# Two forms of the first weights instead of three, and gaps between the operands of the first layer

## The chip, the cores and the metric

The kernel runs on one core of one Trainium2 chip. The metric is the device time of one execution in microseconds (us). An execution under the hardware profiler also gives a span, the time from its first to its last recorded instruction, and the start and the duration of every instruction.

## The reference

A causal convolution over the sequence, with one softmax-normalised kernel of 7 taps for each of 8 heads, and behind it a layer of two matrix products with a hardswish between them. Everything is float32.

```python
# x (8, 4096, 192), weight (8, 7), w_in (192, 2048), w_out (2048, 192)
w = softmax(weight, axis=-1)
y = causal_conv(x, w).reshape(32768, 192)     # 7 taps, one w row per head
h = y @ w_in                                  # 32768 x 2048
g = h * clip(h + 3, 0, 6) / 6
out = g @ w_out                               # 32768 x 192
```

## The kernel before

The 32768 tokens are worked through in 32 blocks of 1024. A block has a convolution (VectorE, ScalarE and a DMA that adds), a **first layer** (`y @ w_in` and the gate) and a **second layer** (`g @ w_out`, done with sums and products of half matrices in place of some of the plain products). In the steady state TensorE does the first layer of a block, then its second layer, then the next block's first layer; the convolution and the splitting of the next block go on beside it.

**The first layer's products.** A tile `y` has 64 channels in its lower 64 partitions for one half of the tokens and the same 64 channels in its upper 64 partitions for the other half, three such thirds `s` side by side, 512 tokens each. So one step of the contraction is a *pair* of matmuls, `k = 0, 1`, one on rows 0 to 63 and one on rows 64 to 127 of TensorE's array, each with its own weights load (64 rows by 128 columns) and 512 columns of `y`. `products` (L437) issues them.

The matmuls run in float32r, a float32 form that goes once over the columns. To keep float32's accuracy both operands are split: `high_of` (L424) writes `y * CUT` in float32r, `low_of` (L427) the rest of it; for the weights, `Rounding.part` (L226) writes `high` (ScalarE, `sig * CUT`), `full` (GpSimd, a cast of `sig`) and `low` (GpSimd, `sig - high`). Three passes then make one product: weights HIGH with columns HIGH, LOW with HIGH, and FULL with LOW (`PASSES`, L28). A *unit* (L465) is one tile of 128 hidden channels for 1024 tokens: 3 passes by 3 thirds by 2 = 18 matmuls, then `relu` on ScalarE (L316) and `gate` on VectorE (L320). A block has 16 units, so 288 matmuls or 144 pairs. Units 0 to 7 take their columns from `y_own`, units 8 to 15 from `y_other`, a copy of `y_own` with the two halves of the partitions exchanged, which four DMAs of SyncE's queue make (`swap`, L303).

**The tiles.** `w_in_parts` (L122) are three tiles of 8 x 3 x 128 floats to a partition (12,288 bytes each). `y_own` are two tiles, HIGH and LOW, of 3 x 512 floats (6,144 bytes each), and `y_other` is one tile with the same two inside it. In the program's allocation they begin at 82,080, 94,368 and 106,656 (weights), 159,648 and 165,792 (`y_own`) and 171,936 (`y_other`) bytes into the partition: each of them is 160 modulo 256, and so is each step by `c`, `s` or part inside them, since 512, 2,048 and 6,144 are multiples of 256. The tag `other` serves `z_other`, three sums of the second layer (L656), in turn with `y_other`. The last tile ends 64 bytes short of the end of the partition.

**Where the weights are made.** At the start, 16 `Rounding` units turn the float64 bits of `w_in` and `w_out` into float32. Eight of them, the ones for `w_in`, end in `part`. This runs beside the first layer of block 0, up to about 62 us.

**The second layer** (`second_layer`, L559) issues float32 matmuls of 256 or 512 columns on the four column groups of the array, each with a weights load of 32 columns (`matmul`, L582).

Of the kernel before, what the change touches and what calls it, by code (L numbers as in the profile page):

```python
# [11 lines left out]
F32 = mybir.dt.float32  # L12
# [5 lines left out]


CUT = 1.0 - 2.0**-13  # L20
HIGH, LOW, FULL = range(3)

PASSES = (HIGH, HIGH), (LOW, HIGH), (FULL, LOW)  # L28


@with_exitstack
def kernel(
# [8 lines left out]
    nc = tc.nc  # L41
    P = nc.NUM_PARTITIONS
# [6 lines left out]
    N = 512  # L49
# [3 lines left out]
    K3 = D // D2  # L53
# [7 lines left out]
    NP = NC // 2  # L61
# [5 lines left out]
    cst = ctx.enter_context(tc.tile_pool(name="cst", bufs=1))  # L67
    xs = ctx.enter_context(tc.tile_pool(name="xs", bufs=1))
    ys = ctx.enter_context(tc.tile_pool(name="ys", bufs=1))
    yo = ctx.enter_context(tc.tile_pool(name="yo", bufs=1))  # L70
# [23 lines left out]
    for base, dma in ((0, nc.scalar), (D2, nc.sync)):  # L94
        dma.dma_start(
            out=w_sb[base : base + D2],
            in_=weight.unsqueeze(1).to_broadcast([H, GJ, KC]),
# [21 lines left out]
    nc.vector.memset(zeros, 0.0)  # L119


    w_in_parts = [cst.tile([P, NP, K3, P], F32, name=f"w_in{n}") for n in range(3)]  # L122
    def own_tiles(name):
        return [yo.tile([P, K3, N], F32, name=f"{name}{n}", tag=f"y{n}") for n in range(2)]

    sm = yo.tile([P, 1], F32, name="sm")
    y_own, z_early = own_tiles("y"), []

    def other_tile():
        return yo.tile([P, 2, K3, N], F32, name="y_other", tag="other")  # L130

    y_other = [other_tile()]
    w_out = cst.tile([P, NP, 7, DH], F32, name="w_out")
    B11, B12, B21, B22, T1, T2, T4 = range(7)
# [38 lines left out]
    class Rounding:  # L173
# [51 lines left out]

        def part(self):  # L226
            if len(self.dst) > 1:
                high, low, full = self.dst
                nc.scalar.mul(r32(high), self.sig[:], CUT)
                nc.gpsimd.tensor_copy(out=r32(full), in_=self.sig[:])  # L230
                nc.gpsimd.tensor_tensor(  # L231
                    out=r32(low), in0=self.sig[:], in1=high, op=ALU.subtract
                )

    def r32(ap):
        return ap.bitcast(F32R)
# [21 lines left out]
    for n in range(5):  # L258
# [7 lines left out]
        out=e_sb[:], in0=w_sb[:], in1=mx[:].to_broadcast([P, KC]), op=ALU.subtract  # L266
# [9 lines left out]
    y = ys.tile([P, K3, N], F32, name="y")  # L276
    OWN, OTHER = range(2)

    def conv_units(i, parts, cuts=1):


        x = x_tiles.pop(i)
        W = N // cuts

        def tap(part, k, t):
            c = c_sb[:, k : k + 1]
            to = y[:, part, t : t + W]
            if k == 0:
                nc.vector.tensor_scalar(
                    out=to, in0=x[:, part, t : t + W], scalar1=c, scalar2=None, op0=ALU.mult  # L290
                )
            else:
                nc.vector.scalar_tensor_tensor(
                    out=to, in0=x[:, part, k + t : k + t + W], scalar=c, in1=to,
                    op0=ALU.mult, op1=ALU.add,
                )

        return [
            lambda part=part, k=k, t=t: tap(part, k, t)
            for part in parts for k in range(KC) for t in range(0, N, W)  # L300
        ]

    def swap(to, part):  # L303
        nc.sync.dma_start(out=to[D2:P], in_=part[0:D2])
        nc.sync.dma_start(out=to[0:D2], in_=part[D2:P])
# [118 lines left out]
    def high_of(out, x):  # L424
        nc.scalar.mul(r32(out), x, CUT)

    def low_of(out, x, high, engine):  # L427
        engine.tensor_tensor(out=r32(out), in0=x, in1=high, op=ALU.subtract)
# [3 lines left out]
    def swap_parts(thirds=slice(0, K3)):  # L432
        y_other[0] = other_tile()
        for n in range(2):
            swap(y_other[0][:, n, thirds], y_own[n][:, thirds])

    def products(n, slot, s, steps=range(3), begin=False, end=False):  # L437
        group, c = divmod(n, NP)
        for m_ in steps:
            wn, yn = PASSES[m_]  # L440
            for k in range(2):
                r = slice(k * D2, (k + 1) * D2)
                nc.tensor.matmul(  # L443
                    out=psum[:, 2 * slot + k], lhsT=r32(w_in_parts[wn][r, c, s]),
                    rhs=r32(y_other[0][r, yn, s] if group else y_own[yn][r, s]),
                    start=begin and m_ == 0, stop=end and m_ == 2, skip_group_check=True,
                )

# [14 lines left out]
    def first_layer(i, jobs):  # L463

        def unit(n):  # L465
            slot = free_slots.pop(0)
            for m_ in range(3):
                for s in range(K3):
                    products(n, slot, s, (m_,), s == 0, s == K3 - 1)
            to, both = places(n, slot)  # L470
            relu(to, both)
            gate(to, both)
            free_slots.append(slot)
# [50 lines left out]
    TH = N // 2  # L524
# [34 lines left out]
    def second_layer(i, between):  # L559
        last = i + 1 == NB  # L560
        ours = [free_slots.pop(0) for _ in range(3)]
        d, e, b, c, a, x_ = (psum[:, 2 * n + k] for n in ours for k in range(2))
# [87 lines left out]
        f, h = ends  # L650
# [2 lines left out]
        A2, B2, C2 = a[second, lo], a[third, lo], a[first, lo]  # L653
        T_2, T_4 = x_[second], e[first]
        A, B, V = f[fourth], h[fourth], b[fourth]
        z_other = yo.tile([P, 3, NP // 2, TH], F32, name="z_other", tag="other")  # L656
        sums_a12 = z_other[:, 0], z_other[:, 1], z_other[:, 2], z[:, :, 1]

        def sum_a12(n):
# [44 lines left out]
        t = clock[2]  # L704
# [204 lines left out]
    with tc.manual_schedule():  # L909
# [4 lines left out]
            out=c_sb[:], in0=e_sb[:], in1=sm[:].to_broadcast([P, KC]), op=ALU.mult  # L914
# [3 lines left out]
        thirds = [slice(s, s + 1) for s in range(K3)]  # L918
# [10 lines left out]
        b, b1 = (2 * free_slots[-1] + k for k in range(2))  # L929
        for _ in range(3):  # L930

            nc.tensor.matmul(  # L932
                out=psum[:, b], lhsT=zeros[:, 0:P], rhs=zeros, start=True, stop=True
# [10 lines left out]
        def thirds_of(n, *which, end=False):  # L944
            if n not in early:
                early[n] = free_slots.pop(0)
            for s in which:
                products(n, early[n], s, begin=s == pe_third, end=end)

        def high_y(s, of):  # L950
            high_of(y_own[HIGH][:, thirds[s]], of)
            swap(y_other[0][:, HIGH, thirds[s]], y_own[HIGH][:, thirds[s]])

        def low_y(s, of):
            low_of(y_own[LOW][:, thirds[s]], of, y_own[HIGH][:, thirds[s]], nc.vector)
            swap(y_other[0][:, LOW, thirds[s]], y_own[LOW][:, thirds[s]])

        def all_of(s):
            return y[:, thirds[s]]
# [7 lines left out]
        for u in conv0[5 : per - 3]:  # L967
            u()
        join(0)
        high_y(pe_third, psum[:, b : b + 1])  # L970
        part(0)
        for u in conv0[per - 3 : per]:
            u()
        low_y(pe_third, psum[:, b : b + 1])
        high_y(0, all_of(0))
        low_y(0, all_of(0))
        thirds_of(0, pe_third, 0)
        thirds_of(NP, pe_third)
        split(1)
        clamp(1)  # L980
        for u in conv0[per + 2 : per + 2 * pe_taps]:
            u()
        add(y[:, 1], psum[:, b1], y[:, 1])
        high_y(1, all_of(1))
        join(1)
        part(1)
        low_y(1, all_of(1))
        for n in (5, 6, 7, 8):
            load(n)
# [36 lines left out]
        for r in range(2 * NP):  # L1026
            k = order[r]
            if k in early:
                slot = early[k]
                if k == NP:  # L1030
                    thirds_of(k, 1, end=True)
            else:
                slot = free_slots.pop(0)
                for m_ in range(3):
                    for s in range(K3):
                        products(k, slot, s, (m_,), s == 0, s == K3 - 1)
            to, both = places(k, slot)
            relu(to, both)
            n = joins.get(r)
# [62 lines left out]
        begin_block_two()  # L1102
        direct_out(0, *third)
        swap_parts()
        w_sums(((T3, B22, B12),))
        last = ctx.enter_context(tc.tile_pool(name="last", bufs=1, reuse_waits="tile"))
# [6 lines left out]
        for i in range(1, NB):  # L1113
            jobs = dict(zip((3, 6, 9, 12), ([job] for job in conv[3:7])))
            jobs[-1] = left
            if i > 1 and conv:

                jobs[-1] = left[:2] + conv[1:2] + left[2:]
                jobs[1] = conv[2:3]
            first_layer(i, jobs)  # L1120
            for job in conv[7:]:
                job()
            conv = []

            def begin_conv():
                x_tiles[i + 2] = load_x(i + 2)
                conv.extend(conv_jobs(i + 2, True))

            between = []
            if i + 1 < NB:  # L1130
                between = [(52.4, split_high), (63, split_rest), (64.2, swap_parts)]
            if i + 2 < NB:
                between += [(40, begin_conv), (65, lambda: conv[0]())]
            left = second_layer(i, between)
# [33 lines left out]
```

## Time and profile before

| | us |
|---|---|
| time, median of 3 runs | 2195.64 |
| lowest and highest of the 3 | 2195.4, 2195.95 |
| time of the profiled execution | 2195.4 |
| its span | 2193.6 |
| TensorE busy | 2185.0 (100%) |
| TensorE's weight loads busy | 1564.3 (71%) |
| VectorE busy | 1979.9 (90%) |
| ScalarE busy | 1271.8 (58%) |
| GpSimd busy | 1018.1 (46%) |

Line numbers (L443) are those of the kernel before. `PE` is TensorE's matmuls, `PEld` its weight loads, `DVE` VectorE, `ACT` ScalarE, `POOL` GpSimd, `SP` SyncE. In a line of groups, the last figures are the busy time, the mean duration of one in ns, and the idle time of the engine just before, with what ended it. A matmul's duration includes its way through the array, so durations of neighbours overlap; how fast the matmuls go is read from the distance between their starts.

### The profile page before, as it was taken

Reading aid. Unit: us, or ns where it says so; the run is one execution under the profiler, and the core shown is the slowest. Engines: PE = TensorE matmul, PEld = TensorE weight load, DVE = VectorE, ACT = ScalarE, POOL = GpSimd, SP = SyncE. Lnnn points to the kernel's source line nnn. Section 1 sums busy time; section 2 is a strip of 40 time slices with the busy share of each in tenths; the row PEclk is TensorE's granted clock in tenths of the full one; section 3 lists DMA queues with packets and bytes.
Section 4 is the critical chain, followed back from the end, with each engine's and each line's share of the span. In section 5 each row is a group of like instructions: output and inputs, shape, how many; then the busy total and the mean of one; then the engine's idle time right before and its main releaser. Section 6 shows DMA issues by size and latency. Waiting matters only on the chain.

```text
span 2193.6 us, 53710 instructions
## 1 busy us (share of the span) xinstructions
PE 2185.0 (100%) x23086; PEld 1564.3 (71%) x23086; DVE 1979.9 (90%) x1871; ACT 1271.8 (58%) x1761; POOL 1018.1 (46%) x867
## 2 busy tenths in 40 slices
PE   9999999999999999999999999999999999999998
PEld 5577777777777777777777777777777777777776
DVE  8889899889899898998989988999999999898987
ACT  7456565565655665555656556565566555565644
POOL 4545543355433555334554335553355543455433
PEclk9999999999999999999999999999999999999999
DMA  7366556756567665666655675656666566765564
GB/s 166 66 120 98 97 99 111 128 90 107 97 111 121 103 109 91 110 112 120 98 97 100 112 127 90 107 98 112 121 106 106 91 110 112 122 97 97 99 105 64
DMA packets 329821, 231.80 MB, mean 106 GB/s; under 512 B 208816, under 2 KB 293296, under 8 KB 329584
## 3 DMA queue, kind: packets, MB, share of 16 engines
q0 software_dynamic: 98752, 122.35, 36.6%
q1 hardware_dynamic: 229320, 105.73, 23.8%
q8 instruction: 181, 2.97, 0.6%
q10 hardware_dynamic: 1512, 0.30, 0.1%
q14 instruction: 56, 0.46, 0.1%
HBM read 31.72 MB, written 25.17 MB: 26 GB/s over the span
## 4 chain that ended last, share of the span: by engine, by line
PE 98%; ACT 1%; DVE 0%; POOL 0%; DMA 0%; issue 0%; POOLq 0%; DVEq 0%
PE psum L583 49%; PE psum L443 47%; PE psum L331 2%; PE psum L924 0%; PE psum L932 0%; ACT g L316 0%; DVE results L410 0%; DMA y_other<-y 0%; POOL w_in L231 0%; ACT scale L207 0%; POOL out_dram L357 0%; ACT sig L204 0%; ACT sig L210 0%; POOL sig L221 0%; DVE xt L833 0%
## 5 line engine op out<-in xcount | busy, mean ns | idle before, releaser
L583 PE MATMUL psum<-g,w_out 128*32 128x512 f32 (+1 forms) x5720 | 1023.8, 508 | 0.0
L316 ACT ACTIVATE g<-psum,half 128x1024 f32<-128x1024 f32 x512 | 571.5, 1116 | 312.4 <-PE psum L443 311.2
L583 PE MATMUL psum<-s,w_out 128*32 128x512 f32 (+1 forms) x3272 | 735.5, 570 | 0.9 <-DVE results L410 0.9
L320 DVE SCALAR_TENSOR_TENSOR g<-g,psum 128x1024 f32<-128x1024 f32 x512 | 609.4, 1212 | 133.1 <-ACT g L316 132.8
L541 POOL TENSOR_TENSOR s<-g 128x256 f32<-128x256 f32 x248 | 254.3, 1025 | 751.3 <-DMA out_dram<-results 538.5
L583 PEld LDWEIGHTS psum<-g,w_out 128*32 128x32 f32 x5720 | 421.4, 110 | 171.1 <-issue 61.6
L443 PE MATMUL psum<-y,w_in 64*128 64x512 f32 x4608 | 534.3, 388 | 0.3
L443 PE MATMUL psum<-y_other,w_in 64*128 64x512 f32 x4608 | 529.0, 386 | 0.0
L443 PEld LDWEIGHTS psum<-y,w_in 64*128 64x128 f32 x4608 | 428.6, 184 | 120.7 <-issue 26.0
L443 PEld LDWEIGHTS psum<-y_other,w_in 64*128 64x128 f32 x4608 | 431.6, 184 | 91.0 <-DMA y_other<-y 0.4
L1007 DVE SCALAR_TENSOR_TENSOR y<-x,c_sb,y 128x1536 f32<-128x1536 f32 x156 | 306.1, 1962 | 1.9 <-ACT y L1004 1.8
L583 PEld LDWEIGHTS psum<-s,w_out 128*32 128x32 f32 x3272 | 227.9, 110 | 106.6 <-issue 54.3
L583 PE MATMUL psum<-g,w_s 128*32 128x256 f32 x1488 | 289.3, 379 | 0.0
L390 POOL TENSOR_TENSOR s<-g 128x1024 f32<-128x1024 f32 x93 | 236.9, 2717 | 0.4 <-DVE g L320 0.4
L583 PE MATMUL psum<-z,w_s 128*32 128x256 f32 x992 | 235.1, 380 | 0.0
L390 DVE TENSOR_TENSOR s<-g 128x1024 f32<-128x1024 f32 x124 | 188.9, 1543 | 1.1
L583 PEld LDWEIGHTS psum<-g,w_s 128*32 128x32 f32 x1488 | 149.8, 110 | 32.0
L583 PE MATMUL psum<-s,w_s 128*32 128x256 f32 x744 | 170.7, 379 | 0.0
L483 ACT ACTIVATE z<-g 128x512 f32<-128x512 f32 x186 | 142.6, 767 | 18.5 <-DVE g L320 18.5
L410 DVE TENSOR_TENSOR g<-g 128x1024 f32<-128x1024 f32 x124 | 143.6, 1220 | 1.1
L410 DVE TENSOR_TENSOR results<-psum,results 32x256 f32<-32x256 f32 (+2 forms) x221 | 107.9, 488 | 39.1 <-PE psum L583 33.8
L541 POOL TENSOR_TENSOR s<-s,g 128x256 f32<-128x256 f32 x124 | 136.4, 1100 | 9.7
(115 smaller groups left out, 2347.8 us busy)
## 6 DMA issues: line engine op xcount, KB each, us to landing
y_other<-y SPq DMA_DIRECT2D x124, 384.0 KB, 5.1
z<-g POOLq DMA_DIRECT2D x93, 512.0 KB, 5.6
z<-z POOLq DMA_DIRECT2D x62, 512.0 KB, 5.4
out_dram<-results SPq DMA_DIRECT2D x375, 64.0 KB, 2.6
y<-x POOLq DMA_DIRECT2D x30, 768.0 KB, 8.9
x<-in_x_dram SPq DMA_DIRECT2D x53, 388.5 KB, 7.4
g<-g POOLq DMA_DIRECT2D x31, 512.0 KB, 6.4
g<-in_moe_w_in_dram SPq DMA_DIRECT2D x16, 192.0 KB, 5.5
```

Of the source, the lines that this page charges most:

```text
L316: nc.scalar.activation(r6, h, ACT.Relu, bias=half[:], scale=1.0 / 6.0)
L320: nc.vector.scalar_tensor_tensor(out=g_, in0=g_, scalar=1.0, in1=h, op0=ALU.min, op1=ALU.mult)
L331: lambda p=p: nc.tensor.matmul(out=bank[j * QS : (j + 1) * QS, tokens], lhsT=w_out[:, p, w, cols], rhs=x[:, p, tokens], start=(first and p ...
L390: engine.tensor_tensor(out=o[:, r], in0=a[:, r], in1=b[:, r], op=op)
L410: nc.vector.tensor_tensor(out=out, in0=x, in1=y, op=op)
L443: nc.tensor.matmul(out=psum[:, 2 * slot + k], lhsT=r32(w_in_parts[wn][r, c, s]), rhs=r32(y_other[0][r, yn, s] if group else y_own[yn][r, s ...
L483: nc.scalar.mul(to, x, sign)
L541: engine.tensor_tensor(out=o, in0=p, in1=q, op=op)
L583: nc.tensor.matmul(out=out, lhsT=w, rhs=x, start=start, stop=True, tile_position=(0, j * QS), skip_group_check=True,)
L1007: nc.vector.scalar_tensor_tensor(out=y[:], in0=taps_of(k), scalar=c_sb[:, k : k + 1], in1=y[:], op0=ALU.mult, op1=ALU.add,)
```

## The change

The third form of `w_in` goes: HIGH becomes the plain float32r copy of `sig` (no factor CUT), LOW is `sig - HIGH` as before, and the third pass takes HIGH where it took FULL. The cast on GpSimd (L230) is left out. Nothing changes in how `y` is split, in the number, order and shapes of the matmuls, or in the queues.

Padding tiles are put between the operands: 128 bytes between the two weight tiles, 192 ahead of `y0`, 64 ahead of `y1`, 64 ahead of `y_other`, and 64 between the two parts of `y_other`. With 12,288 bytes less and 128 more ahead of them, `y0`, `y1` and the two parts of `y_other` begin 64, 128, 192 and 0 bytes ahead of HIGH's weights modulo 256; LOW's weights begin 128 after HIGH's. All tiles behind the weights move: `w_out` by 12,160 bytes, which is 128 modulo 256.

```diff
-HIGH, LOW, FULL = range(3)
+HIGH, LOW = range(2)
...
-PASSES = (HIGH, HIGH), (LOW, HIGH), (FULL, LOW)
+PASSES = (HIGH, HIGH), (LOW, HIGH), (HIGH, LOW)
...
-    w_in_parts = [cst.tile([P, NP, K3, P], F32, name=f"w_in{n}") for n in range(3)]
+    def gap(pool, name, size):
+        if size:
+            pool.tile([P, size // 4], F32, name=name)
+
+    w_in_parts = [cst.tile([P, NP, K3, P], F32, name="w_in0")]
+    gap(cst, "gap_w", 128)
+    w_in_parts.append(cst.tile([P, NP, K3, P], F32, name="w_in1"))
...
-    y_own, z_early = own_tiles("y"), []
+    gap(yo, "gap_y0", 192)
+    y_own = [yo.tile([P, K3, N], F32, name="y0", tag="y0")]
+    gap(yo, "gap_y1", 64)
+    y_own.append(yo.tile([P, K3, N], F32, name="y1", tag="y1"))
+    z_early = []
+    gap(yo, "gap_other", 64)
+    OTHER_GAP = 16
+
+    def other_words(name):
+        return yo.tile([P, 2 * K3 * N + OTHER_GAP], F32, name=name, tag="other")
 
     def other_tile():
-        return yo.tile([P, 2, K3, N], F32, name="y_other", tag="other")
+        words = other_words("y_other")
+        return [
+            words[:, b : b + K3 * N].rearrange("p (s n) -> p s n", n=N)
+            for b in (0, K3 * N + OTHER_GAP)
+        ]
...
-                high, low, full = self.dst
-                nc.scalar.mul(r32(high), self.sig[:], CUT)
-                nc.gpsimd.tensor_copy(out=r32(full), in_=self.sig[:])
+                high, low = self.dst
+                nc.scalar.copy(out=r32(high), in_=self.sig[:])
...
-            swap(y_other[0][:, n, thirds], y_own[n][:, thirds])
+            swap(y_other[0][n][:, thirds], y_own[n][:, thirds])
...
-                    rhs=r32(y_other[0][r, yn, s] if group else y_own[yn][r, s]),
+                    rhs=r32(y_other[0][yn][r, s] if group else y_own[yn][r, s]),
...
-        z_other = yo.tile([P, 3, NP // 2, TH], F32, name="z_other", tag="other")
+        z_other = other_words("z_other")[:, : 3 * NP // 2 * TH].rearrange(
+            "p (k u t) -> p k u t", u=NP // 2, t=TH
+        )
```

More of the change, by code (lines that the diff above doesn't have):

```diff
@@ L951, in high_y @@
             high_of(y_own[HIGH][:, thirds[s]], of)
-            swap(y_other[0][:, HIGH, thirds[s]], y_own[HIGH][:, thirds[s]])
+            swap(y_other[0][HIGH][:, thirds[s]], y_own[HIGH][:, thirds[s]])
         def low_y(s, of):
             low_of(y_own[LOW][:, thirds[s]], of, y_own[HIGH][:, thirds[s]], nc.vector)
-            swap(y_other[0][:, LOW, thirds[s]], y_own[LOW][:, thirds[s]])
+            swap(y_other[0][LOW][:, thirds[s]], y_own[LOW][:, thirds[s]])
         def all_of(s):
```

## The prediction

> **What bounds the kernel.** First the page: who is busy, and what the chain of waits runs along.
>
> ```profile
> span 2193.6 us, 53710 instructions
> PE 2185.0 (100%) x23086; PEld 1564.3 (71%) x23086; DVE 1979.9 (90%) x1871; ACT 1271.8 (58%) x1761; POOL 1018.1 (46%) x867
> ...
> PE 98%; ACT 1%; DVE 0%; POOL 0%; DMA 0%; issue 0%; POOLq 0%; DVEq 0%
> PE psum L583 49%; PE psum L443 47%; PE psum L331 2%; PE psum L924 0%; PE psum L932 0%; ACT g L316 0%; DVE results L410 0%; DMA y_other<-y 0%; POOL w_in L231 0%; ACT scale L207 0%; POOL out_dram L357 0%; ACT sig L204 0%; ACT sig L210 0%; POOL sig L221 0%; DVE xt L833 0%
> ```
>
> The chain lies on TensorE for 98% of the span, and 47% of it is L443, the first layer's matmuls, which are the ones that the change touches. So the time changes by what the distance between those matmuls changes, and by little else. The chain in order of time gives that distance by stage (start, length, matmuls):
>
> ```profile
> 162.10 32.86 PE psum L443 x288
> 194.97 34.61 PE psum L583 x304
> ```
>
> A first layer is 144 pairs in 32.86 us, 228.2 ns a pair. Inside it, away from its beginning, the busy time by stretches says
>
> ```profile
> 170.00:190.40 20.40, 20.40 (x184) 16.86 (x182) 1.00 0.39 55
> ```
>
> 20.40 us hold 184 matmuls, of which about 4 are cut by the edges: 90 pairs, **226.7 ns a pair** at a granted clock of 1.00. Read to the ns from their starts, the pairs 6 to 144 of blocks 1 to 31 are 226 or 227 apart without one exception, mean 226.67. In these stretches VectorE, ScalarE, GpSimd and the DMA queues come and go, so what sets 226.67 lies inside TensorE and its own reads. Is it the least? The second layer's float32 matmuls, which pass over their columns more slowly, have this spacing in one of the four streams:
>
> ```profile
> 402.50 0.38 PE L583 MATMUL psum<-z,w_s 128*32 128x256 f32 x1
> ...
> 402.72 0.38 PE L583 MATMUL psum<-z,w_s 128*32 128x256 f32 x1
> ...
> 404.01 0.38 PE L583 MATMUL psum<-z,w_s 128*32 128x256 f32 x1
> ```
>
> Seven steps of 256 columns in 1.51 us, 215.7 each. The first layer's form takes 226.67 for 512 columns, so it is about twice as fast, but not quite: if twice were its floor, 11 ns of each pair would be lost. The first pairs of a block show that the loss isn't constant. Their starts in the trace (mean over blocks 1 to 31) are 336.7, 235.8, 228.3, 232.5 and 230.8 ns apart, the same in every block, and only then 226.67 for good. The loss depends on how the pair's columns and the weights loaded meanwhile stand to each other in time, and it settles into one rhythm. In the kernel before all five operands begin at 160 modulo 256 (front part), so the rhythm is the same in all passes and both groups.
>
> **The change, part by part.**
>
> The cast on GpSimd goes. Its row and its neighbours, eight of each:
>
> ```profile
> L231 POOL TENSOR_TENSOR w_in<-sig,w_in 128x384 fp32r<-128x384 f32 x8 | 8.9, 1113 | 8.7 <-ACT w_in L229 8.7
> ...
> L230 POOL CAST w_in<-sig 128x384 fp32r<-128x384 f32 x8 | 4.4, 551 | 0.5
> ...
> L229 ACT ACTIVATE w_in<-sig 128x384 fp32r<-128x384 f32 x8 | 4.1, 514 | 1.8 <-POOL sig L221 1.8
> ```
>
> 4.4 us of GpSimd's work. The subtraction L231 behind it waits for ScalarE's HIGH anyway: 8.7 us of idle time, 6 times of the 8. In the other two, cast and HIGH end within 0.1 us of each other (14.19 and 14.10 us; 21.00 and 20.97). So L231 starts at most 0.1 us earlier, twice. TensorE waits for L231 1.1 us and for L229 1.1 us in all; I take 0, bounds -0.2 and, if the copy should be slower than the scaled copy it replaces (577 ns for the nearest copy, L580 over 512 columns, against 514 for 384: 63 ns twice), +0.2 us.
>
> The tiles move. No instruction is added: 9,216 matmuls and weights loads, the same DMAs (`swap`, 124 issues of 384 KB on SP), one wait for each as before. `y_other` is one tile still, so its DMAs have the same predecessors. For the second layer, `w_out` moves by 128 modulo 256 against `g`. Its rows speak against any cost: with `g` (0 from `w_out` modulo 256) and with `s` (32 from it) the same matmul has the same mean.
>
> ```profile
> L583 PE MATMUL psum<-g,w_out 128*32 128x512 f32 x3456 | 870.6, 592 | 0.0
> L583 PE MATMUL psum<-s,w_out 128*32 128x512 f32 x2928 | 728.1, 592 | 0.0
> ```
>
> I take 0 there, and 0 for the other engines, whose operands only move. If I am wrong by 1 ns for each of the about 80 steps of 430 ns in a block's second layer, that is 0.08 us a block, 2.5 us.
>
> What remains is the spacing of 4,608 pairs (9,216 / 2). Four steps between columns and weights take the place of one: HIGH columns of `y_own` stand 64 ahead of HIGH weights and 192 ahead of LOW, its LOW columns 128; those of `y_other` 192, 64 and 0. The trace of before has only 0, so the price is bounded from both sides:
> - fastest: every pair at the float32 stream's 215.7 ns: (215.7 - 226.7) x 4,608 = -50.7 us, 2144.7 against the profiled 2195.4
> - slowest: every pair at the worst settled-in distance seen, 235.8: +9.1 x 4,608 = +42 us, 2237.
>
> Which value? Of the 18 pairs of an own and an other unit 15 come to a step that isn't 0, and 3 (LOW columns of `y_other`) stay at 0. I take the middle between the float32 floor and the present distance for all pairs, 221.2 ns, since some steps will be better than others and the third pass of `y_other` won't move: -5.5 x 4,608 = -25 us. **2195.4 - 25 = 2170 us**; the median of the runs shown is 0.2 above the profiled one, which is nothing here.
>
> Would something else then set the end? Busy time by stretches, first and second layer of one block (PE, PEld, DVE, ACT, POOL):
>
> ```profile
> 162.10:194.97 32.87, 32.87 (x293) 26.91 (x296) 29.45 (x25) 22.64 (x23) 23.25 (x22) 1.00 0.48 73
> 194.97:229.58 34.61, 34.61 (x434) 22.08 (x434) 31.81 (x33) 16.68 (x31) 7.48 (x6) 1.00 0.77 140
> ```
>
> VectorE, the next, has 29.45 of 32.87 us. At 221.2 ns a first layer takes 0.8 us less, at the floor 1.6: 31.3 us, which still holds 29.45. A gate comes every 9 x 221.2 = 1.99 us and takes 1.21. So the gain isn't taken back, though at the floor only 1.8 us are left.
>
> **Rivals.**
>
> *The step between the operands makes no difference.* Then the 11 ns belong to the pair itself (two row groups at once, the change of weights), and the time stays within 1 us of 2195.4. For: all 139 settled pairs of a block are alike to the ns whatever `c`, `s` and pass. Against: all those have the same step, so they can't tell; and the first pairs show that the loss moves between 1.6 and 9.1 ns above the settled one with nothing but timing changed. The Trainium skill gives this rival a mechanism: "TensorE: Matmul & The Clock Gate", Part 2, on the weights load, has two independent read ports for columns and weights, so that loading the next weights takes nothing from the running matmul. By it the change does nothing, 2195.4. The float32 rows agree with it (215.7 with loads under way), the 226.67 of the first layer doesn't say. Chance 0.14.
>
> *The rhythm is lost* (the other side). The settled 226.67 is less than any of the four distances ahead of it. It takes four pairs to reach, and needs each pair to repeat the one before. After the change the step changes at each pass, every three pairs: 64, 192, 128, then 64 again. If each change throws the pairs back to the four unsettled distances, they never settle: their mean (235.8 + 228.3 + 232.5 + 230.8) / 4 = 231.9, +5.2 x 4,608 = +24 us, **2219 us**. If only the first three count, (235.8 + 228.3 + 232.5) / 3 = 232.2, 2221. It decides as soon as the mean over the nine pairs of a unit is above 226.67. For: settling is plainly there, and takes longer than a pass. Against: the unsettled pairs follow a start at which the loads were out of time (106 ns behind the matmul, later 3), not a change of address. Chance 0.40.
>
> *The change doesn't do what it says*: the paddings could be dropped or rounded so that steps stay 0. By the sizes in the code they come out at 64, 128, 192 and 0. Counted with the first rival, 0.01.
>
> **From this to the numbers.** Faster through better steps 0.45; no effect 0.15; rhythm lost 0.40. A measurement of this kernel tells about 0.2% (4.4 us) from no change. The likeliest, faster, has its own range 2144 to 2190, with 2170 in it. Over all: the faster cases above 2140, the unchanged ones, and the slower ones up to a little above 2221 leave out about 2 in 10, most of it the part of the lost rhythm nearer to 2237: 2140 to 2225. Faster by over 0.2%: 0.45; within: 0.15; slower: 0.40.
>
> **What will show it.** The chain's first-layer pieces: 32.1 us in place of 32.86 if I am right, 33.6 if the rhythm is lost, 32.86 if nothing matters. The starts of L443 by pass: own units in passes 1 and 2 (64, 192), pass 3 (128), other units the same with 192, 64 and 0; the passes at 0 should keep about 226.7, the others fall toward 216. The second layer's pieces must stay 34.61. VectorE's waits must not turn up ahead of TensorE's loads of L443. I am wrong if passes at steps other than 0 take 227 or more.

## The result and the profile after

| | before | after |
|---|---|---|
| median, us | 2195.47 (5 runs, 2195.39 to 2195.95) | 2220.45 (5 runs, 2220.40 to 2220.63) |
| ratio | | 1.0114, 95% interval 1.0102 to 1.0125 |
| span of the profiled execution, us | 2193.6 | 2218.7 |

The kernel became 25 us slower. The time lies in the range that was given, but on the other side of the forecast of 2170. The page of the kernel after, with the shares of the engines and the chain by line (the matmuls of the first layer are now L463, those of the second L603):

```profile
span 2218.7 us, 53702 instructions
PE 2210.0 (100%) x23086; PEld 1567.2 (71%) x23086; DVE 1972.1 (89%) x1871; ACT 1274.7 (57%) x1761; POOL 1020.0 (46%) x859
...
PE 99%; DVE 0%; POOL 0%; DMA 0%; ACT 0%; issue 0%; POOLq 0%; DVEq 0%
```

TensorE sets the time as before, with the same 23,086 matmuls. The chain in order of time (start, length, matmuls) says where the 25 us are:

```profile
163.22 33.66 PE psum L463 x288
196.88 34.61 PE psum L603 x303
231.49 33.66 PE psum L463 x288
```

A second layer takes 34.61 us, to the digit what it took. A first layer takes 33.66 in place of 32.86: 0.80 us more, 31 times, 24.8 us. No other engine has become the limit. By stretches of one block (PE, PEld, DVE, ACT, POOL):

```profile
163.22:196.88 33.66, 33.66 (x292) 26.93 (x296) 29.38 (x25) 22.77 (x23) 23.41 (x22) 1.00 0.49 75
196.88:231.49 34.61, 34.61 (x434) 22.13 (x434) 31.60 (x33) 16.66 (x31) 6.87 (x5) 1.00 0.74 136
```

VectorE has 29.38 us of work in the first stretch, as before (29.45); the granted clock is 1.00. So the same matmuls are further apart. In the stretch where the kernel before had 184 of them there are now fewer:

```profile
170.00:190.40 20.40, 20.40 (x178) 16.52 (x176) 1.00 0.39 57
```

Read from the starts in the trace, the distance from each pair to the next in the nine pairs of a settled unit, one away from the beginning of a block and of a group (ns, from the first matmul of a pair to the first of the next, mean over blocks 2 to 31, counted from 0; the order is pass 1, 2, 3 with three thirds each):

```
                 pass 1               pass 2               pass 3         sum
before           226.7 226.6 226.7    226.7 226.6 226.7    226.7 226.6 226.7   2040.0
after, own       225.8 225.8 235.8    230.8 235.8 231.7    234.2 229.2 237.5   2086.7
after, other     234.2 235.8 231.7    236.7 231.6 233.4    225.8 235.8 228.3   2093.3
```

The mean of an own unit is 231.85 ns, of an other unit 232.6. The series repeats from unit to unit, and from block to block, within 1.3 ns of its mean. In both kernels the second matmul of a pair starts 3 to 5 ns after the first, so that one distance serves for both.

The cast that was taken out left no trace in the time. The subtraction behind it now waits for ScalarE's HIGH for all of the time that it gained:

```profile
L251 POOL TENSOR_TENSOR w_in<-sig,w_in 128x384 fp32r<-128x384 f32 x8 | 8.5, 1060 | 14.4 <-ACT w_in L250 14.4
...
L250 ACT CAST w_in<-sig 128x384 fp32r<-128x384 f32 x8 | 4.0, 506 | 2.3 <-POOL sig L242 2.3
```

### The profile page after: what moved, and what is told of

Its sections match the earlier page's. It is cut to its first block, busy times and chain, and to the rows that moved or that the text cites. A ratio compares the mean times of both kernels' runs of the same rounds, so it can differ in the third digit from the quotient of the medians.

```text
span 2218.7 us, 53702 instructions
## 1 busy us (share of the span) xinstructions
PE 2210.0 (100%) x23086; PEld 1567.2 (71%) x23086; DVE 1972.1 (89%) x1871; ACT 1274.7 (57%) x1761; POOL 1020.0 (46%) x859
## 4 chain that ended last, share of the span: by engine, by line
PE 99%; DVE 0%; POOL 0%; DMA 0%; ACT 0%; issue 0%; POOLq 0%; DVEq 0%
PE psum L463 48%; PE psum L603 48%; PE psum L351 2%; PE psum L946 0%; PE psum L954 0%; DVE results L430 0%; DMA y_other<-y 0%; POOL out_dram L377 0%; DVE xt L855 0%; POOL sig L242 0%; POOL p L818 0%; DVE s L410 0%; POOL w_in L251 0%; DVE y L313 0%; POOLq L1185 0%
## 5 line engine op out<-in xcount | busy, mean ns | idle before, releaser
L603 PE MATMUL psum<-g,w_out 128*32 128x512 f32 (+1 forms) x5720 | 1023.7, 508 | 0.0
L603 PE MATMUL psum<-s,w_out 128*32 128x512 f32 (+1 forms) x3272 | 735.6, 570 | 0.9 <-DVE results L430 0.9
L561 POOL TENSOR_TENSOR s<-g 128x256 f32<-128x256 f32 x248 | 246.8, 995 | 754.1 <-DMA out_dram<-results 665.7
L463 PE MATMUL psum<-y,w_in 64*128 64x512 f32 x4608 | 546.7, 393 | 0.2
L603 PEld LDWEIGHTS psum<-g,w_out 128*32 128x32 f32 x5720 | 421.2, 110 | 171.5 <-issue 62.1
L463 PE MATMUL psum<-y_other,w_in 64*128 64x512 f32 x4608 | 542.2, 391 | 0.0
L463 PEld LDWEIGHTS psum<-y,w_in 64*128 64x128 f32 x4608 | 429.2, 184 | 132.2 <-issue 26.7
L463 PEld LDWEIGHTS psum<-y_other,w_in 64*128 64x128 f32 x4608 | 432.1, 184 | 103.9 <-DMA y_other<-y 0.4
L603 PEld LDWEIGHTS psum<-s,w_out 128*32 128x32 f32 x3272 | 227.8, 110 | 105.7 <-issue 53.8
L603 PE MATMUL psum<-g,w_s 128*32 128x256 f32 x1488 | 289.3, 379 | 0.0
L603 PE MATMUL psum<-z,w_s 128*32 128x256 f32 x992 | 235.1, 380 | 0.0
L410 DVE TENSOR_TENSOR s<-g 128x1024 f32<-128x1024 f32 x124 | 181.7, 1485 | 1.1
L603 PEld LDWEIGHTS psum<-g,w_s 128*32 128x32 f32 x1488 | 149.9, 110 | 31.9
L603 PE MATMUL psum<-s,w_s 128*32 128x256 f32 x744 | 170.7, 379 | 0.0
L561 POOL TENSOR_TENSOR s<-s,g 128x256 f32<-128x256 f32 x124 | 150.2, 1211 | 9.7
```

What stands on the lines that cost most here:

```text
L410: engine.tensor_tensor(out=o[:, r], in0=a[:, r], in1=b[:, r], op=op)
L463: nc.tensor.matmul(out=psum[:, 2 * slot + k], lhsT=r32(w_in_parts[wn][r, c, s]), rhs=r32(y_other[0][yn][r, s] if group else y_own[yn][r, s ...
L561: engine.tensor_tensor(out=o, in0=p, in1=q, op=op)
L603: nc.tensor.matmul(out=out, lhsT=w, rhs=x, start=start, stop=True, tile_position=(0, j * QS), skip_group_check=True,)
```

## The experiments

The kernels are the changed one with other paddings (the last ones with other loads too). Each was run once; the kernel before, run beside them, took 2195.6 to 2195.9. "Step" is how far the columns of a running pair begin ahead of the weights, modulo 256 bytes. At first three theories stood against each other: that a change of step from pass to pass costs (A, the rival of the lost rhythm), that the steps cost in themselves (B), and that some other step is better than 0 (C).

**Two forms, no gaps.**

```diff
-    gap(cst, "gap_w", 128)
+    gap(cst, "gap_w", 0)
...
-    gap(yo, "gap_y0", 192)
+    gap(yo, "gap_y0", 0)
...
-    gap(yo, "gap_y1", 64)
+    gap(yo, "gap_y1", 0)
...
-    gap(yo, "gap_other", 64)
-    OTHER_GAP = 16
+    gap(yo, "gap_other", 0)
+    OTHER_GAP = 0
```

> Two forms of w_in as in the change, all gaps 0, so that every step between columns and weights is 0 modulo 256 again. If the gaps are the whole cause: settled pairs 226.7 ns apart, time 2195.5 within 1. If the second form's reuse of HIGH in the third pass (the same weights read in two passes) or the moved tiles cost anything: pairs of the third pass above 226.7, time up to 2220.

2195.39 us, span 2193.6, which is the span of before. The first layer in the chain is back:

```profile
162.15 32.86 PE psum L463 x288
195.01 34.61 PE psum L603 x304
```

All settled pairs are 226.7 ns apart. So the two forms, the missing cast and the moved tiles cost nothing and bring nothing; the gaps are the whole cause.

**One step for all passes.** `gap_w`, `gap_y1` and `OTHER_GAP` are 0, so that both weight tiles and both parts of the columns have one step in a group:

```diff
+    gap(yo, "gap_y0", 64)       # second kernel: 128
...
+    gap(yo, "gap_other", 128)   # second kernel: 160
```

> Two forms, one step for all passes of a group: own columns 64 ahead of both weight tiles, other columns 192 ahead. Theory A (the change of step from pass to pass breaks the rhythm): pairs settle within about 5 at 226.7 ns in both groups, time 2195 to 2197. Theory B (the steps 64 and 192 are slow in themselves): settled distances of 231 to 233 ns, time 2217 to 2223. Theory C (another step is better than 0): one of the groups settles below 226.7, time below 2190.

> As the run before with own columns 128 ahead and other columns 32 ahead. Theory A: both groups settle at 226.7 ns, time 2195 to 2197. Theory B: 231 to 233 ns at 128 (32 isn't in the change), time above 2205. Theory C: one of them below 226.7.

2224.02 and 2224.49 us: theory A falls, since nothing changes from pass to pass here and the first layers are longer than in the change. The chain of the first of the two kernels:

```profile
163.23 33.79 PE psum L463 x285
197.02 34.61 PE psum L603 x304
```

Away from 0 the pairs do settle, but not on one distance: they run through a series that repeats. At 64 it is 225.8, 229.2, 231.7 (mean 228.9); at 192 it is 230.8 and 235.8 in turn (233.3); at 128 a series of seven (232.4); at 32 one of four (233.3).

At 64 and 128 this is the series of the first matmul of a pair alone. The second one, on the other half of the rows, runs at 233.3 ns in the mean. At 64 it so falls 4.4 ns further behind with each pair, and in the seventh own unit it is a whole pair late. From there on it starts after the first matmul of the next pair: the last matmul of a unit, which signals ScalarE, stands one place later in the order of starts. At the end of the own units it is 319 ns behind the first of its pair. Why the two part wasn't found.

**Only the gap between the weights.**

```diff
     gap(cst, "gap_w", 128)
...
-    gap(yo, "gap_y0", 192)
+    gap(yo, "gap_y0", 128)
...
-    gap(yo, "gap_y1", 64)
+    gap(yo, "gap_y1", 0)
...
-    gap(yo, "gap_other", 64)
-    OTHER_GAP = 16
+    gap(yo, "gap_other", 0)
+    OTHER_GAP = 0
```

> Only the gap between the two weight tiles is left (128 bytes): all columns 0 ahead of HIGH's weights, 128 behind LOW's. The step changes twice in the nine pairs of a unit. Theory A: no settling, a mean of 229 to 232 ns over the nine pairs of a unit, time 2206 to 2220. Theory B with 0 good and 128 bad: only the second pass slow, the time a third of the way, about 2203.

2217.85 us. Both groups have the same nine distances:

```
                       pass 1               pass 2               pass 3              sum
gap_w only             226.7 226.7 232.5    240.8 232.5 235.8    228.3 232.5 230.8   2086.7
before, pairs 2 to 6 of a block:                235.8    228.3 232.5 230.8 | 226.7
```

The three distances that break out, 232.5, 240.8, 232.5, begin with the *last* pair of pass 1, whose own weights and columns are at step 0. It is the pair during which the first weights of LOW are loaded: in the trace of the kernel before, the load for the next pair starts 2.5 to 3.4 ns after a settled pair does. So the weights count one pair ahead of their own: what counts is the **weights loaded meanwhile**. That the columns are those of the running pair, this run can't show; the run with 240 and 16 does. And the four distances behind them are, to the tenth, the four of a block's start: once off, the pairs at step 0 need four more to come back. Of the 46.7 ns that a unit loses, 25.8 are in the three pairs at step 128 and 20.7 in the four that come back. The time lies in theory A's range, and for the second of these two parts A's reason holds.

**More steps.** The same layout with own and other columns at further steps. For steps that aren't multiples of 32 a tile is made a little longer and begun a few words in:

```diff
-            for b in (0, K3 * N + OTHER_GAP)
+            for b in (9, K3 * N + OTHER_GAP + 9)
...
+    def w_in_tile(name):
+        words = cst.tile([P, NP * K3 * P + 2], F32, name=name)
+        return words[:, 2:].rearrange("p (c s f) -> p c s f", c=NP, s=K3)
```

> One step for all passes: own columns 96 ahead of both weight tiles, other columns 160. Theory A (only the change of step costs) has fallen with the steps 64, 192, 128 and 32. Theory D (the distance depends on the step between a pair's columns and the weights loaded meanwhile, and only near 0 do the pairs repeat one short distance): both groups run in repeating series of several distances with means of 228 to 234 ns, time 2207 to 2226. Theory E (the distance is a fixed price of the step, periodic and symmetric about 0): 96 as 160, between the 233.3 of 32 and the 232.4 of 128, time 2223 to 2225.

> Own columns 224 ahead of the weights (32 behind), other columns 4 ahead. Theory D: 224 in a series with a mean of 228 to 234 ns; 4 settles on one distance, 225 to 229 ns. Theory E, symmetric: 224 as 32, 233.3 ns, and 4 at 227 to 228. A step a little off 0 that beats 0 would show as other units under 226.7 ns.

> Own columns 8 behind the weights (248), other columns 8 ahead. Theory D: each settles on one distance near 226.7, or falls into a series with a mean up to 234, and the two needn't be alike. Theory E: both the same, a little above 226.7. Either below 226.7 would beat the kernel before.

> Own columns 16 behind the weights (240), other columns 16 ahead. Theory D: not alike, means of 222 to 234 ns. Theory E: both alike, between 226.7 and 233.3, about 230.

2226.38, 2235.18, 2219.14 and 2200.14 us. The means of settled units are in the table below. The worst is a step of 4 bytes, 238.5 ns; the chain of that kernel has the longest first layer of all:

```profile
163.87 34.14 PE psum L463 x288
198.00 34.61 PE psum L603 x304
```

Theory E (a price symmetric about 0) falls: 8 bytes ahead cost 233.3 and 8 behind 230.7, 16 ahead 228.4 and 16 behind 226.9. Of theory D the dependence on the step stands. That the pairs repeat one short distance near 0 doesn't: at 4, 8 and 248 they run through series with means of 238.5, 233.3 and 230.7, where its guess for 4 was 225 to 229. At 240 (16 behind) the own units run at 226.7 in 29 of the blocks 1 to 31 and at 233.3 in two of them, 1 and 6. So there are two rhythms at this step, and which one comes can differ between blocks of one run.

The same run shows which columns count. Where the columns turn from own to other, the weights stay at one place modulo 256. In the 29 settled blocks the last own pair still takes 225 to 227 ns, though the next pair has the other columns; only the distance behind it, the first with other columns running, breaks out to 231 to 233. So it is the step between the *running* columns and the weights loaded meanwhile.

**Two steps that settle, in turn.** All gaps are set so that the columns are at 0, and only the tile of LOW's weights is begun 16 bytes later:

```diff
+    w_in_words = cst.tile([P, NP * K3 * P + 4], F32, name="w_in1")
+    w_in_parts.append(w_in_words[:, 4:].rearrange("p (c s f) -> p c s f", c=NP, s=K3))
```

> All columns 0 ahead of HIGH's weights and 240 ahead of LOW's (only LOW's weights are moved, by 16 bytes). Each of these two steps settles when it stands alone, at 226.7 and 226.9 ns. Theory A' (a change of step costs in itself, whatever the steps): nine pairs of a unit at a mean of 229 to 232 ns, time 2206 to 2220. Theory D (only the step of each pair counts, and where the raster stands when it comes): if both steps leave the raster where it was, 226.7 to 227, time 2195 to 2198.

2196.45 us. Here the first layer's matmuls are L464:

```profile
162.18 32.90 PE psum L464 x288
195.08 34.61 PE psum L604 x304
```

The step changes twice in each unit, and from the twelfth of a block on the pairs are 226.7 ns apart. A change between these two steps costs nothing by itself. What it brought to the first layer, 0.04 us, is that settling at a block's start takes 11 pairs in place of 5.

**The last multiples of 16.**

> Own columns 48 ahead of both weight tiles, other columns 208. Of the steps so far only 0 and 240 settle on one distance. Theory D: series with means of 226 to 236 ns. A step that beats 226.7 would have to show here or in the next run if it is a multiple of 16; I expect none, and a time of 2205 to 2226.

> Own columns 112 ahead of both weight tiles, other columns 176: the same question. None below 226.7, time 2205 to 2226.

2222.65 and 2221.55 us. The steps 80 and 144 weren't tried. Means of settled units, ns (units 2 to 7 for own columns, 10 to 15 for other, of blocks 2 to 31; at 64 and 128, where the two matmuls of a pair part, first and second by themselves):

```
step   0      4      8      16     32     48     64           96     112
mean   226.7  238.5  233.3  228.4  233.3  232.6  228.9/233.3  233.3  233.3
step   128          160    176    192    208    224    240    248
mean   232.5/233.3  234.3  232.0  233.3  233.3  233.3  226.9  230.7
```

At 48 two rhythms take turns, 233.3 in the odd blocks and 231.9 to 232.0 in the even ones. At 16 the other units of block 1 ran at 226.7. No step tried beats 0, and none of these kernels beats the one before.

**Half of each load.** To see whether the loads' reads hold up the running pair, loads of 64 columns; half of the hidden channels is left out:

```diff
-    gap(cst, "gap_w", 128)
+    gap(cst, "gap_w", 0)
...
-    gap(yo, "gap_y0", 192)
+    gap(yo, "gap_y0", 0)
...
-    gap(yo, "gap_y1", 64)
+    gap(yo, "gap_y1", 0)
...
-    gap(yo, "gap_other", 64)
-    OTHER_GAP = 16
+    gap(yo, "gap_other", 0)
+    OTHER_GAP = 0
...
-                    out=psum[:, 2 * slot + k], lhsT=r32(w_in_parts[wn][r, c, s]),
+                    out=psum[0:D2, 2 * slot + k], lhsT=r32(w_in_parts[wn][r, c, s, 0:D2]),
...
-        for _ in range(3):
+        for bank in (b, b, *range(8)):
             nc.tensor.matmul(
-                out=psum[:, b], lhsT=zeros[:, 0:P], rhs=zeros, start=True, stop=True
+                out=psum[:, bank], lhsT=zeros[:, 0:P], rhs=zeros, start=True, stop=True
```

> The change as it is, but each first-layer matmul loads only the first 64 of its 128 columns of weights and writes only 64 partitions of PSUM; the other half of the hidden channels is left out, and seven more matmuls on zeros stand at the start. If the loads' reads are what holds up the running pair: the mean of a unit falls from 232 towards 216 to 224 ns, and the time falls by 35 to 75 us below 2220. If the pair itself sets its distance, by its columns and the two row groups: 231 to 233 ns as before, time 2220 to 2230.

2212.93 us, some of it the matmuls on zeros at the start; the settled distances tell more. They are 227.1, 231.2, 231.7 in turn, 230.0 in the mean, in all passes and both groups. But the expectation speaks of the change's steps, and in the kernel that ran all gaps are 0, as the edit shows. So 230.0 is the distance of half loads at step 0, to be held against 226.7 and not against 232, and neither of the two expectations was put to the test. The next run is the same kernel once more. Behind it come half loads with 224 and 4, and a whole-load kernel with 192 and 64 exchanged between the groups:

> Half loads again (64 of 128 columns of weights, half of the hidden channels left out, seven more matmuls on zeros), but all steps 0, as in the kernel before. With the changed steps the half loads ran at 227.1, 231.2, 231.7 in turn, mean 230.0, alike in all passes and both groups. If a half load makes the step without effect: the same 230.0 here, time 2213 within 1. If the step still counts: 226.7 or less, time about 2197 to 2205.

> Half loads with the steps 224 (own) and 4 (other), which took 233.4 and 238.5 ns with whole loads. If a half load makes the step without effect: 230.0 in both groups, time 2213 within 1. If not: other units above own units, 232 ns or more, time above 2220.

> Whole loads, one step for all passes as in the run with 64 and 192, but exchanged: own columns 192 ahead, other columns 64. If the step sets the distance: own units at 233.3, other units at 228.9 or 233.3 (64 showed both), time 2220 to 2226. If it is the group (own or other tiles): own units at 228.9 first, other at 233.3, as before the exchange.

2212.89, 2232.04 and 2214.48 us. The first of them gives 230.0 again; that shows only that the kernel repeats itself, not that the step is without effect. With 224 and 4 half loads take 231.7 and 236.3. So the step counts with half loads too. Against whole loads, half loads are 1.6 and 2.2 ns faster at 224 and 4, and 3.3 ns *slower* at step 0. What they do at 64, 128 and 192 was not measured. The chain of the half loads at step 0:

```profile
167.69 33.27 PE psum L463 x288
200.96 34.61 PE psum L603 x304
```

33.27 us against 32.86 with whole loads.

The exchange settles the other question: 192 gives 233.3 in the own units, as it did in the other ones, and 64 gives 228.9 in the other units. The step sets the distance, not the group of tiles. Here the two matmuls of a pair stay within 4 ns of each other, and both run at 228.9 at step 64. The kernel with the same two steps the other way round, where the second matmuls ran at 233.3, took 2224.02: 9.5 us more, as a first layer takes 33.48 us here against 33.79 there.

## Why the prediction was wrong

- *Bound and place.* Right: the time moved by what the distance between the first layer's matmuls moved, 24.8 of 25.0 us; second layer 34.61 us, startup and moved tiles 0 (the run without gaps: the span of before to the tenth).
- *The cast at 0.* Right, for the reason given: L251's wait for ScalarE grew from 8.7 to 14.4 us.
- *The spacing of the 4,608 pairs, -5.5 ns each.* **This term failed**, with its sign: measured +5.2 in own and +5.9 in other units. It rested on two things. One was 215.7 ns, the float32 stream's spacing, as a floor that another step could reach. None of the 17 steps tried came under 226.7 in the mean of a settled unit. The other was that "some steps will be better than others": the settled 226.67 was taken for a loss that the equal residues brought about, where it is the best of all the steps tried. The trace of before had a hint: the four distances ahead of settling are all above 226.67, so that off the rhythm was worse, not better.
- *The lost rhythm, 2219 to 2221.* The number was right to 1.5 us, but by the reason given only a tenth of the loss is accounted for, so that the number is for the greater part luck. The rival said that the change of step throws the pairs back. Steps 0 and 240 in turn cost nothing, and constant steps of 64 and 192 cost as much as the change. Where it does apply is the return to step 0. In an other unit of the change the last three distances, 225.8, 235.8, 228.3, are at step 0 by the weights loaded meanwhile, and the last two are those of a block's start: 3 pairs lose 225.8 + 235.8 + 228.3 - 3 x 226.7 = 9.8 ns. An own and an other unit together lose 46.7 + 53.3 = 100 ns, so the rest, nine tenths, falls in pairs at other steps. By the constant-step means those would lose 6 x (2.2 to 6.6) at 64, 6 x 6.6 at 192 and 3 x 5.7 at 128, 70 to 96 ns in all, where 90 were lost. In the change the two matmuls of a pair stay together, and in the run where they did so at 64 it cost 2.2. By that, some 20 of the 90 ns aren't explained by the steps alone; the change from one to the next may have a part there, which wasn't tested.
- *No effect of the step.* Refuted: how long a running pair takes depends on where the weights loaded meanwhile lie, 226.7 ns at step 0 and 238.5 at step 4. For this form of matmul it doesn't hold, then, that loading the next weights takes nothing from the running matmul ("TensorE: Matmul & The Clock Gate", Part 2, of the Trainium skill); whether it is at the read ports that the two meet isn't shown. For the float32 matmuls of the second layer the rule agrees with the trace: 34.61 us whether `w_out` lies 0 or 128 from `g`.
- *VectorE's slack.* Not put to the test, as TensorE didn't become faster.

Open: through what the columns and the loads meet (a shared bank, a port or a buffer), why half a load is slower at step 0, why the two matmuls of a pair part at 64 in one kernel and not in the other, what decides between the two rhythms at 48 and 240, and what would bring the pairs under 226.7 ns. Only the dependence on the step is shown, and that it is the step between the running columns and the next pair's weights. Moving the columns alone and moving the weights alone both change the distance; step 0 itself was only run with both at 160 modulo 256, so that 160 counts for nothing is not shown.

## What to carry to other kernels

A perfectly even spacing above a guessed floor isn't yet a loss that a layout can win back: look first at what the spacing does where it isn't settled. Here that was worse, and it said on which side a change would fall. Where a layout is to be tried, give each group one constant value and read the settled spacing by group: one run gives two values, and a layout that mixes four tells of none. Read it for both matmuls of a pair, since they can part. And attribute the distance behind a matmul to the weights that are loaded while it runs, not to its own.

## What was not expected of the hardware

- Four bytes matter: the same pairs take 226.7 ns at step 0 and 238.5 at step 4.
- With whole loads, each clean series closes on a multiple of 6.67 ns: 226.67 is 34 of them, 225.8 + 229.2 + 231.7 = 686.7 is 103, 230.8 + 235.8 = 466.7 is 70, the series of four at 32 (933.3) 140, the nine of the changed kernel's own unit (2086.7) 313 and of its other unit (2093.3) 314. With half loads three distances sum to 690.0, which is 103.5.
- In the kernel before and in the changed one the series are the same in all blocks to 1.3 ns, whatever the other engines do beside them. At steps 48 and 240 they aren't: a second rhythm of 233.3 ns (35 times 6.67) turns up there in some blocks.
- The two matmuls of a pair, on two halves of the rows, need not keep together: at step 64 one ran at 228.9 ns and the other at 233.3, and the second came to start after the first of the next pair.
